# Interleaved memory attention and multi-head attention: the kernel without its filler matmuls on TensorE

## The chip, the cores and the metric

The kernel runs on one core of a Trainium2 chip. The metric is the device time in microseconds of one execution, as the median of several runs. The engines have short names here: PE is TensorE, ACT is ScalarE, DVE is VectorE, POOL is GpSimd, SP is SyncE. "The granted clock" is the share of TensorE's full clock that the chip let it have, as the trace records it.

## The reference

Four layers run one after another on x of 2048 tokens by 512 features in bf16: A, B, A, B. Each is a residual block on a layer-normalised input. There are 32 heads of 16 features.

```python
def A(x):                                  # memory attention, 4 segments of 512 tokens
    for s in range(4):
        p = softmax(q_s @ k_s.T * scale + causal_mask)      # inside the segment
        a_dot = p @ v_s
        num, den = phi(q_s) @ M, phi(q_s) @ z + 1e-6        # memory of earlier segments
        o = g * num / den + (1 - g) * a_dot
        M, z = M + phi(k_s).T @ v_s, z + sum(phi(k_s))
    return concat(outs) @ wo

def B(x):                                  # full attention over 2048 keys
    p = softmax(q @ k.T * scale)
    return (p @ v) @ wo

x = x + A(layernorm(x)); x = x + B(layernorm(x))            # layers 1, 2
x = x + A(layernorm(x)); x = x + B(layernorm(x))            # layers 3, 4
```

The work that counts is the exponential: 32 heads by 2048 by 2048 in each B layer, and a quarter of that, less the blocks above the diagonal, in each A layer.

## The kernel before

The program is laid out at build time by a scheduler written in Python. It keeps a modelled time for each engine (`sc.t["pe"]`, `sc.t["act"]`, ...), picks the next piece of work in a loop, and emits it into that engine's instruction stream. On the chip the engines then run their streams and wait for one another by semaphores. The code counts layers from 0, so `L` is 0 to 3.

Scores come in tiles of 128 keys by 512 queries, one PSUM bank each. Three tiles make a group: three matmuls, then one exponential on ACT over 1536 columns into a ring in SBUF (`pT`). Two sets of three banks alternate, so that PE fills one set while ACT reads the other:

```python
    # emit_group (cut)
    sc.add("pe", lambda e: e.matmul(out, lhsT, rhs, start=True, stop=True), ..., name="S",
           cost=((SC0 if k == 0 else N / 2400.0) if i == 0 else SC1),
           cold=N / 2400.0 if i == 0 else 0.0, work=0.14 * N / 512)          # line 1113
    ...
    o = sc.add("act", lambda e: e.activation(dst, src, ACT.Exp, scale=float(SCALE)), ...,
               name="E", cost=0.065 + W / 1200.0)                            # line 1120
```

Part of the score tiles of the B layers, four at a time, go to DVE instead, which works out the exponential in eight steps on 128x2048 after moving each tile out of PSUM (line 1249). Weighted sums of values follow, on line 1376 with the values stationary, and on line 1358 with the probabilities stationary (layers `L` 2 and 3; 17 columns each). All projections, the memory products and the output projections pass through one helper (line 610), mostly as groups of four accumulating matmuls.

The scheduler has a model of PE's clock. It adds up the matmul work in windows of `HAM_W` us, and takes PE to be warm if the window before had at least `HAM_T`; a matmul in a cold window costs more in the model:

```python
HAM_W = 3.4133
HAM_T = 5.0
KEEP = 6.0
KEEP0 = 3.0
KEEP_D = 0.0
KEEP_L = 2
CF = 0.684

    def clock(self, t, work):
        w = int(t / HAM_W)
        if w > self.win:
            self.warm = w == self.win + 1 and self.work >= HAM_T
            self.win, self.work = w, 0.0
        self.work += work
        self.past.append((t, work))
        while self.past[0][0] < t - HAM_W:
            self.past.popleft()
        return self.warm

    # add() (cut)
        if eng == "pe" and not self.clock(t0, work):
            cost += CF * cold
```

When the loop finds nothing ready for PE, it moves PE's modelled time on to the next event. Before it does so, it may put in a filler: a matmul of zeros, added to the accumulation that is open at that moment, so that no result changes. `rs`, `rp` and `rx` are the times at which the next score group, value sum and DVE tile become ready:

```python
    # end of run()'s loop
            to = min(nxt)
            d = 0.23 if sc.warm else 0.44
            tc = min([x for x in (rs, rp, rx) if x is not None], default=to)
            if KEEP and self.acc_open and t + d <= tc + KEEP_D and (0.0 if sc.warm else KEEP0) <= sc.lately() < KEEP and self.pvu and self.pvu[0]["L"] <= KEEP_L:
                self.keep_warm()
                continue
            sc.t["pe"] = to

    def keep_warm(self):

        bank = self.acc_bank
        self.sc.add("pe", lambda e: e.matmul(self.ps[:, bank.col0:bank.col0 + 512], self.zw[:, :], self.wA[:, 0, 0:512], start=False, stop=False,
                                             skip_group_check=True),
                    reads=[self.b_zw, self.b_wA[0]], bank_ops=[(bank, "w", self.acc_alloc)], emit=False, name="D", cost=0.215, cold=0.2133, work=1.0)   # line 1826
```

`sc.lately()` is the work of the last `HAM_W` us. `KEEP_L = 2` keeps fillers out of the last layer.

Of the kernel before, what the change touches and what calls it, by code (L numbers as in the profile page):

```python
# [37 lines left out]
LAST = 3  # L38
HAM_W = 3.4133
HAM_T = 5.0  # L40
KEEP = 6.0
KEEP0 = 3.0
KEEP_D = 0.0
KEEP_L = 2
# [239 lines left out]
class KernelBuilder:  # L284
# [1444 lines left out]
    def run(self):  # L1729
# [3 lines left out]
        while True:  # L1733
# [83 lines left out]
# [3 lines that stand above are left out]
# [80 lines left out]
```

## Time and profile before

| what | value |
|---|---|
| time, median of 3 runs | 2110.33 us (2109.41 to 2111.07) |
| span of the profiled run | 2108.4 us |
| mean granted TensorE clock | 0.670 |
| busy ACT / PE / DVE / POOL | 1996.9 / 1737.0 / 1608.0 / 253.4 us |
| exponentials on ACT (line 1120) | 1504, 1962.6 us |
| score tiles that go to DVE (line 1249) | 420, that is 105 times four |
| filler matmuls (line 1826) | 126, 53.0 us |

A line of the page's groups names the source line, the engine and operation, what it writes and reads, how many there are, then busy time and the mean length of one, and then how long the engine stood idle just before them and who ended that. [...] Layers follow one another, but not sharply: the scheduler mixes units of two layers.

### The profile page before, as it was taken

To read this page: it belongs to the slowest core of one execution; us is meant where nothing else is said; L and a number is where in the kernel's file an instruction comes from. 1 tells how busy PE (TensorE), PEld (TensorE's weight loads), DVE (VectorE), ACT (ScalarE), POOL (GpSimd) and SP (SyncE) were. 2 spreads that over 40 slices of the span, in tenths; PEclk is the share of its full clock that TensorE was granted. 3 is DMA by queue.
4 is the path that set the end of the run, shared out by engine and by line. 5 is a ranking of instruction groups with operands and counts; after the bars stand their busy time and mean duration, and the time that the engine had idled before them with its cause. 6 is when DMAs were issued, how large, how long until landed. Compare 5 with 4: busy or idle time off the path is not lost.

```text
span 2108.4 us, 41713 instructions
## 1 busy us (share of the span) xinstructions
PE 1737.0 (82%) x17508; PEld 597.9 (28%) x17508; DVE 1608.0 (76%) x2449; ACT 1996.9 (95%) x1593; POOL 253.4 (12%) x564
## 2 busy tenths in 40 slices
PE   6879978887878787878888888888888888888887
PEld 2222221112231122221232223213444433434443
DVE  7887558876648768777767678578789878988894
ACT  6869889999999999999999998999999999999998
POOL 4542220000130003110021102200000000000000
PEclk9779876568575796577875797575655555556555
DMA  4210100001000000010000100000000000000000
GB/s 120 51 31 20 22 11 1 1 1 21 1 11 11 6 16 1 1 21 11 11 1 1 19 13 1 14 8 2 14 4 4 4 14 4 4 5 14 5 6 12
DMA packets 75468, 27.33 MB, mean 13 GB/s; under 512 B 68112, under 2 KB 74768, under 8 KB 75280
## 3 DMA queue, kind: packets, MB, share of 16 engines
q1 hardware_dynamic: 74176, 23.62, 5.4%
q8 instruction: 137, 2.24, 0.4%
q10 hardware_dynamic: 1104, 1.05, 0.1%
q14 instruction: 51, 0.42, 0.1%
HBM read 6.30 MB, written 2.10 MB: 4 GB/s over the span
## 4 chain that ended last, share of the span: by engine, by line
ACT 46%; PE 26%; issue 10%; DVE 4%; POOL 1%; DMA 0%; SPq 0%; ACTq 0%; DVEq 0%
ACT pT L1120 45%; PE ps L1113 11%; PE ps L610 6%; PE ps L1358 4%; PE ps L1376 3%; PE ps L1246 1%; POOL pT L1143 1%; DVE dz L1249 1%; DMA xT<-xn 0%; PE ps L1826 0%; ACT et L765 0%; DVE db L1304 0%; DVE dz L1302 0%; DVE db L1293 0%; DVE tokk L1302 0%
## 5 line engine op out<-in xcount | busy, mean ns | idle before, releaser
L1120 ACT ACTIVATE pT<-ps 128x1536 bf16<-128x1536 f32 (+1 forms) x1504 | 1962.6, 1494 | 85.3 <-PE ps L1113 68.8
L1113 PE MATMUL ps<-q,kB 32*128 32x512 bf16 x3676 | 680.4, 535 | 264.5 <-ACT pT L1120 256.4
L1249 DVE TENSOR_SCALAR dz<-ps 128x512 int32<-128x512 f32 x420 | 289.8, 690 | 148.0 <-PE ps L1246 135.7
L1113 PEld LDWEIGHTS ps<-q,kB 32*128 32x128 bf16 x3676 | 129.2, 97 | 691.0 <-ACT pT L1120 645.7
L1143 POOL TENSOR_SCALAR_AFFINE_SELECT pT<-pT 128x256 bf16<-128x256 bf16 (+2 forms) x516 | 224.6, 464 | 544.7 <-ACT pT L1120 543.4
L1376 PE MATMUL ps<-pT,vB 128*17 128x512 bf16 x2228 | 271.3, 491 | 3.8 <-DVE kB L625 1.3
L1246 PE MATMUL ps<-q,kB 32*128 32x512 bf16 x420 | 238.7, 568 | 0.2 <-DVE dz L1249 0.2
L1358 PEld LDWEIGHTS ps<-vB,pT 128*128 128x128 bf16 x5792 | 181.0, 104 | 165.1 <-issue 163.9
L1358 PE MATMUL ps<-vB,pT 128*128 128x17 bf16 x5792 | 213.7, 176 | 0.0
L1113 PE MATMUL ps<-q,kA 32*128 32x128 bf16 (+3 forms) x1024 | 122.2, 381 | 41.9 <-ACT pT L1120 39.6
L1286 DVE TENSOR_SCALAR df<-dz 128x2048 f16<-128x2048 uint16 x105 | 129.2, 1230 | 2.9
L1376 PEld LDWEIGHTS ps<-pT,vB 128*17 128x17 bf16 x2228 | 51.3, 89 | 189.2 <-issue 174.3
L1293 DVE TENSOR_SCALAR db<-dz 128x2048 int16<-128x2048 int16 x77 | 94.3, 1225 | 0.5 <-PE ps L1376 0.5
L1496 DVE STREAM_TRANSPOSE T<-ps 128x512 f32<-128x512 f32 x94 | 66.7, 709 | 28.4 <-PE ps L1376 27.8
L610 PE MATMUL ps<-xT,wB 128*128 128x512 bf16 x256 | 81.5, 452 | 5.3 <-DMA xT<-xn 2.5
L610 PE MATMUL ps<-xT,wA 128*128 128x512 bf16 x256 | 72.5, 412 | 6.0 <-DVE T L1496 2.6
L655 POOL TENSOR_SCALAR lnr<-lnmv 128x4 f32<-128x4 f32 x15 | 6.0, 403 | 565.5 <-DVE lnmv L650 565.5
L976 DVE TENSOR_TENSOR x_tok<-x_tok,ps 128x512 bf16<-128x512 bf16 x60 | 41.0, 686 | 42.6 <-PE ps L610 42.2
L1298 DVE TENSOR_TENSOR tokk<-tokk,df 128x2048 f16<-128x2048 f16 x56 | 68.3, 1220 | 0.8
L1302 DVE TENSOR_TENSOR tokk<-tokk,df 128x2048 f16<-128x2048 f16 x56 | 68.3, 1219 | 0.8
L665 DVE TENSOR_SCALAR xn<-x_tok,lnmv,lnr 128x512 bf16<-128x512 bf16 x60 | 25.3, 442 | 54.6 <-DMA xT<-xn 52.2
L1113 PEld LDWEIGHTS ps<-q,kA 32*128 32x128 bf16 x1024 | 29.8, 99 | 120.8 <-ACT pT L1120 95.3
(130 smaller groups left out, 1613.4 us busy)
## 6 DMA issues: line engine op xcount, KB each, us to landing
x_tok<-in_A_x_dram SPq DMA_DIRECT2D x14, 128.0 KB, 2.7
wB<-in_B_wqkv_dram SPq DMA_DIRECT2D x4, 384.0 KB, 4.4
out_dram<-x_tok SPq DMA_DIRECT2D x3, 512.0 KB, 3.6
xT<-xn SPq DMA_TRANSPOSE x60, 2.4
wA<-in_A_wk_dram SPq DMA_DIRECT2D x1, 512.0 KB, 5.5
wA<-in_A_wq_dram ACTq DMA_DIRECT2D x1, 512.0 KB, 6.8
wA<-in_A_wv_dram SPq DMA_DIRECT2D x1, 512.0 KB, 7.0
woA<-in_A_wo_dram SPq DMA_DIRECT2D x1, 512.0 KB, 6.8
```

Of the source, the lines that this page charges most:

```text
L610: return self.sc.add("pe", lambda e: e.matmul(out, lhsT, rhs, start=start, stop=stop), reads=reads, bank_ops=[(bank, "w", alloc)], emit=la ...
L1113: sc.add("pe", (lambda out, lhsT, rhs: lambda e: e.matmul(out, lhsT, rhs, start=True, stop=True))(out, lhsT, rhs), reads=reads, bank_ops=[ ...
L1120: o = sc.add("act", lambda e: e.activation(dst, src, ACT.Exp, scale=float(SCALE)), writes=[self.b_pT[s0 + i] for i in range(n)], bank_ops= ...
L1143: om = sc.add("pool", (lambda ap, pat: lambda e: e.affine_select(ap, ap, pattern=pat, compare_op=ALU.is_ge, fill=0.0, base=0, channel_mult ...
L1246: sc.add("pe", lambda e: e.matmul(out, lhsT, rhs, start=True, stop=True), reads=reads, bank_ops=[(bank, "w", alloc)], emit=True, name="SX" ...
L1249: o = sc.add("dve", lambda e: e.tensor_scalar(dst, out, float(EXP_C * 65536.0), -126.0 * 65536.0, op0=ALU.mult, op1=ALU.max), writes=[self ...
L1286: o = dv(lambda e: e.tensor_scalar(F, lo, 2.0 ** -16, -0.5, op0=ALU.mult, op1=ALU.add), bz, bF, "dF", 1.24)
L1293: o = dv(lambda e: e.tensor_scalar(E, hi, 128.0, 16256.0 + 53.0, op0=ALU.mult, op1=ALU.add), bz, bE, "dE", 1.24)
L1298: o = dv(lambda e: e.tensor_tensor(Pz, Pz, F, ALU.mult), bF + bP, bP, "dP2", 1.24)
L1302: o = dv(lambda e: e.tensor_tensor(Pz, Pz, F, ALU.mult), bF + bP, bP, "dP4", 1.24)
L1358: op = sc.add("pe", (lambda o0, w, v, first: lambda e: e.matmul(self.ps[:, o0:o0 + 17], w, v, start=first, stop=True, skip_group_check=Tru ...
L1376: sc.add("pe", (lambda out, v, rhs, start, stop: lambda e: e.matmul(out, v, rhs, start=start, stop=stop, skip_group_check=True))(out, v, r ...
```

## The change

One constant is changed: `KEEP`, the amount of recent work up to which fillers are put in, goes from 6.0 to zero. The condition is then never met and no filler is emitted. The version after is described as: layer 3 memory attention queries-stationary, wide query masks, four Z sums early, projection of the last segment accumulated early, new unit order. All of that stands in both kernels; the fillers, which are for keeping PE's clock up in the first three layers, are the whole difference in the source. The scheduler runs with the same rules and all its other constants, on a PE timeline that has no fillers in it.

```diff
--- before.py
+++ after.py
@@ -38,7 +38,7 @@
 LAST = 3
 HAM_W = 3.4133
 HAM_T = 5.0
-KEEP = 6.0
+KEEP = 0.0
 KEEP0 = 3.0
 KEEP_D = 0.0
 KEEP_L = 2
```

## The prediction, made before the result was known

> **What bounds the kernel now.** I read the page first: the busy shares, then the strip of 40 slices. ScalarE (ACT) is busy for 1996.9 us of 2108.4; nothing else is near it.
>
> ```profile
> PE 1737.0 (82%) x17508; PEld 597.9 (28%) x17508; DVE 1608.0 (76%) x2449; ACT 1996.9 (95%) x1593; POOL 253.4 (12%) x564
> ...
> PE   6879978887878787878888888888888888888887
> ...
> ACT  6869889999999999999999998999999999999998
> ...
> PEclk9779876568575796577875797575655555556555
> ```
>
> The ACT strip is at 9 from slice 7 on (from about 320 us), while the granted TensorE clock swings between full and half in slices 7 to 25 and lies at half from slice 29 to the end, with ACT still at 9. So the clock, which is all that the filler matmuls are there for, does not by itself set the pace. The loss is in 111 us of ACT idle time, so next I read the groups of ACT by shape and the waits.
>
> ```profile
> L1120 ACT ACTIVATE pT<-ps 128x1536 bf16<-128x1536 f32 x1312 | 1800.3, 1559 | 62.9 <-PE ps L1113 49.7 <-POOL pT L1143 5.9 <-PE ps L1246 4.9
> ```
>
> ```profile
> PE ps L1113 <- ACT pT L1120: 295.9, 726, 1.5
> ...
> ACT pT L1120 <- PE ps L1113: 68.8, 64, 10.1
> ```
>
> PE waits for ACT 726 times and ACT for PE 64 times. Those 64 waits are what a warmer or colder PE can change. The last view is of the object of the change, the filler of line 1826, alone, and then of whole stretches of 50 us (columns: span of the stretch, busy us and count of PE, PEld, DVE, ACT, POOL, then granted clock, DMA share, GB/s).
>
> ```profile
> L1826 PE MATMUL ps<-wA,zw x126: 376/390/634, 113.3 to 1294.5; 128*128 128x512 bf16 x126
> ```
>
> ```profile
> 400.00:450.00 50.00, 41.09 (x255) 7.69 (x251) 43.79 (x55) 49.94 (x39) 0.00 (x0) 0.53 0.00 1
> ...
> 750.00:800.00 50.00, 39.62 (x302) 12.05 (x301) 35.31 (x74) 50.00 (x43) 3.59 (x5) 0.95 0.04 9
> ...
> 1600.00:1650.00 50.00, 42.47 (x655) 20.65 (x651) 45.28 (x56) 50.00 (x38) 0.00 (x0) 0.50 0.02 4
> ```
>
> There are 126 fillers, all between 113 and 1295 us; 71 ran at the full clock and 55 at half (durations under and over 450 ns). The stretch 750 to 800 us has 17 of them, the most of any, and ACT has no gap in it: fillers can sit beside the work for nothing. The stretch 400 to 450 us has 5, and the clock is 0.53 all the same. The stretch 1600 to 1650 us has none, the clock is at half, and ACT has no gap either.
>
> [...] its clock record holds only 0.50 and 1.00, changing on a grid of 3.413 us. [...] the trace has medians of 379 ns for warm projection matmuls and 602 ns for the score matmuls (mostly cold)[...]. [...] the trace shows 78 of them without a gap in 105.54 us (from 611 us on), so 1353 ns each. That last number is the kernel's beat: three score tiles in 1.353 us of ACT.
>
> **The change part by part.** With KEEP at zero the branch that emits the filler is never taken.
>
> *Removed:* 126 matmuls of 512 columns. In a row, four projection matmuls start 658 / 3 = 219 ns apart at full clock and 1252 / 3 = 417 ns at half (median first-to-fourth start distances of the groups of line 610). So the fillers hold the array for 71 x 0.22 + 55 x 0.42 = 38.7 us. PE was waiting for ACT 296 us in the whole run, and the scheduler puts a filler only where its own model shows an empty slot. The chain that ended last has 0.5% (10 us) on line 1826, but much of this lies in stretches where ACT has no gap, like 750 to 800 us; there nothing is gained. I take 1 to 2 us as the direct gain.
>
> *Lost:* warm windows. For every window of 3.413 us I added up the matmuls of the trace, a full 128x128 matmul of 512 columns counting as 1 and the others by their share of array and columns (the 17-column ones of line 1358 left out). Under 4, the next window was warm in 2 of 352 cases; from 4 to 6 in 51 of 110; over 6 in 151 of 152. Fillers stand in 63 windows. Without them 45 of the 63 fall below 4.5, and 28 of these were followed by a warm window. So some 28 windows, or 96 us, may go cold: the mean granted clock would fall from 0.670 by 96 x 0.5 / 2108 = 0.023, to about 0.647. What counts is what runs in those 28 windows: 6 projection groups of four. Each takes 1252 - 658 = 594 ns longer, 3.6 us of PE in sum. How much of that reaches ACT? Around 1346 us a cold group (1.89 us) before a score group makes the exponential wait 0.88 us, and this 0.88 comes back many times; about half of the cold groups show no such gap. From 340 to 1295 us 17 of 98 groups are cold, and ACT is idle 24.3 us from all causes. So 6 x 0.88 x 0.5 to 6 x 0.88, that is 2.6 to 5.3 us, and as much as 1 us for the memory products of lines 610 (136 columns) in those windows. I take 4 us as the direct loss.
>
> *Moved:* the program's order. Scheduling is done at build time against a model of each engine, which counts a cold matmul dearer, so once the first filler is gone (113 us) every later choice may fall otherwise: which of two ready units comes first, when a projection is squeezed in, how many quadruples of score tiles go to VectorE (now 105). One quadruple more or less is 4 x 1.353 / 3 = 1.8 us of ACT. The 10.08 us wait near 141 us, and those of 4.5 us near 310 us, 4.1 us near 802 us and 3.0 us near 913 us, sit at joints between segments and can each shrink or grow. The other constants (unit order, rate, look-ahead) are shared by both kernels. If they were chosen for the present order, a shuffle more often hurts than helps; I book +2 us, with a spread of about 10.
>
> *Sum:* 2110.3 - 1.5 + 4 + 2 = about **2115 us**.
>
> **The rivals.**
> *Fillers in the way.* Each cold filler is 0.42 us ahead of a score group in PE's program order. If the 10 us that the chain puts on line 1826 were all delay, the change would give 2100. For it: the model's clock is not the chip's, and 55 fillers ran at the slow price though the model hoped for the fast one. Against it: 726 waits of PE for ACT, and no ACT gap in the stretch with most fillers.
> *The clock is worth more than I count.* If each window that the fillers warm keeps the next warm too, perhaps 20 instead of 6 projection groups turn cold, and memory products and layer normalization wait for them at the joints: 20 x 0.88 = 18 us, so 2128. Against it: in most of the 28 windows no projection follows at all, and the projections bring their own activity (four in one window are already 4 of the 5 that the scheduler asks for).
> *Only the shuffle.* Clock and fillers cancel and the new order decides, by one or two quadruples and one joint: 2095 to 2130, either sign.
>
> **Range and chances.** The direct terms are a few us; the shuffle gives the width. I take 2098 to 2132 us for 8 in 10. Two per cent is 42 us: more than a third of all ACT idle time won, or that much lost. Winning it needs ACT work to shrink as well, so 1% for faster, 4% for slower, 95% for within 2%.
>
> **What would show it.** Right: line 1826 is gone; the mean clock falls to 0.63 to 0.66, with slices 7 to 25 lower; ACT busy time stays within 6 us of 1996.9; ACT's waits on line 1113 grow by 2 to 8 us from 68.8; the count of L1249 stays near 420. Wrong: an ACT idle time that shrinks at a lower clock would speak for fillers in the way; a changed L1249 count with ACT busy following at 1.8 us for each four, for the shuffle; many new waits of 0.88 us behind line 610, for the dearer clock. A whole new wait at a joint, over 5 us, would be a miss that I can't foresee from this trace.

## The result and the profile after

The changed kernel takes 2093.86 us (2089.86 to 2096.14) against 2110.7 us: a ratio of 0.9915, with a 95% interval of 0.9896 to 0.9935. It is faster by 0.85%, some 18 us. The prediction was 2115 us in a range of 2098 to 2132, so both the sign and the range were wrong; the 95% given to a change within 2% held.

The page of the changed kernel, busy shares and strips:

```profile
PE 1732.3 (83%) x17382; PEld 589.3 (28%) x17382; DVE 1605.0 (77%) x2447; ACT 1997.3 (95%) x1595; POOL 248.1 (12%) x563
...
ACT  5879989999999999999999999999999999999998
...
PEclk9779876567565575576765788575655565555555
```

ACT does the same work as before, 1997.3 us against 1996.9, in a span that is 14 us shorter (2094.3 against 2108.4). PE has 126 matmuls less and its clock fell from 0.670 to 0.643, as foreseen. So all that was won is ACT idle time. The exponentials over 1536 columns, which before stood behind 62.9 us of idle time, and ACT's longest waits:

```profile
L1120 ACT ACTIVATE pT<-ps 128x1536 bf16<-128x1536 f32 x1312 | 1800.4, 1551 | 52.7 <-PE ps L1113 46.3 <-POOL pT L1143 1.7 <-PE ps L1246 1.7
```

```profile
ACT pT L1120 <- PE ps L1113: 59.3, 59, 6.8
...
ACT pT L1120 <- POOL pT L1143: 4.7, 6, 2.1
```

The count stays (1312), the idle time falls by 10 us, and the longest wait is 6.8 us, in the first 20 us of the program, where it was 10.1, at the first joint. The stretches of 50 us (same columns as in the prediction):

```profile
400.00:450.00 50.00, 41.60 (x259) 7.27 (x255) 45.65 (x55) 49.93 (x39) 0.00 (x0) 0.50 0.00 1
750.00:800.00 50.00, 40.72 (x306) 11.41 (x306) 36.46 (x77) 49.94 (x42) 6.02 (x16) 0.66 0.04 9
1600.00:1650.00 50.00, 42.09 (x660) 20.72 (x657) 45.04 (x55) 49.94 (x38) 0.00 (x0) 0.50 0.02 5
```

From 750 to 800 us the clock is 0.66 in place of 0.95, and ACT is as full as before (49.94 us busy against 50.00). Where, then, do the 18 us come from? The next table follows the progress of ACT: for each share of all exponential columns, the time at which it was done in the two traces. The difference moves in steps, not evenly:

| time in the kernel before, us | 46 | 125 | 210 | 281 | 768 | 834 | 1259 | 1394 | 2100 |
|---|---|---|---|---|---|---|---|---|---|
| changed minus before, us | +2.9 | +4.7 | -0.3 | -4.1 | -4.0 | -8.3 | -7.1 | -16.0 | -15.6 |

There are three steps, of about 9, 4 and 9 us, with little between them and nothing in the last 700 us, where neither kernel has fillers. A second trace of the changed kernel (run e9 below) has the same three steps, of about 10, 4 and 9 us. The first two are joints: places where an output projection or a quadruple of DVE tiles has to be finished before the next unit goes on. The third is not one long wait. Its stretch of work, in the kernel before and then in the changed one (columns: span of the stretch, busy us and count of ACT, granted clock, DMA share, GB/s):

```profile
1259.00:1394.00 135.00, 121.21 (x109) 0.68 0.05 10
```

```profile
1252.00:1378.00 126.00, 120.32 (x108) 0.76 0.05 10
```

ACT is idle 13.8 us of it before and 5.7 us after. The longest wait shrinks only from 4.10 to 3.29 us; of the shorter waits, nine of 0.3 us and more become two. Among these, five of about 0.88 us, the length that the prediction tied to cold projection groups, become two. The changed kernel, without fillers, has the higher clock here. The first joint on ACT in the kernel before (start, length, instruction, idle time before it and who ended it):

```profile
138.10 0.63 ACT L765 ACTIVATE et<-tokk 128x512 bf16<-128x512 bf16 x1 [2.03 <-DVE sm L899]
140.76 0.63 ACT L765 ACTIVATE et<-tokk 128x512 bf16<-128x512 bf16 x1 [2.03 <-DVE sm L899]
151.47 2.37 ACT L1120 ACTIVATE pT<-ps 128x1536 bf16<-128x1536 f32 x2 [10.08 <-PE ps L1113]
```

And in the changed kernel:

```profile
138.84 1.02 ACT L1120 ACTIVATE pT<-ps 128x1024 bf16<-128x1024 f32 x1 [3.28 <-PE ps L1113]
...
145.47 0.63 ACT L765 ACTIVATE et<-tokk 128x512 bf16<-128x512 bf16 x1 [2.32 <-DVE sm L899]
149.82 3.71 ACT L1120 ACTIVATE pT<-ps 128x1536 bf16<-128x1536 f32 x3 [3.72 <-PE ps L1113]
```

Here the scheduler must finish the output projection of segment 0 before it can reuse a buffer, and issues no scores until that is done. In the plan (the modelled order and times that the scheduler works out) that takes eight steps of its threads in the old order and five in the new; a 10 us hole becomes two of under 4 us.

The second joint, all engines, in the kernel before:

```profile
794.88 0.38 PE L1246 MATMUL ps<-q,kB 32*128 32x512 bf16 x1
...
796.03 1.23 DVE L1286 TENSOR_SCALAR df<-dz 128x2048 f16<-128x2048 uint16 x1
...
804.18 0.39 PE L1376 MATMUL ps<-db,vB 128*17 128x512 bf16 x4 [2.43 <-DVE db L1304]
...
806.36 2.79 ACT L1120 ACTIVATE pT<-ps 128x1536 bf16<-128x1536 f32 x2 [4.12 <-POOL pT L1143]
```

And in the changed kernel:

```profile
782.19 0.63 PE L1246 MATMUL ps<-q,kB 32*128 32x512 bf16 x1
...
783.59 1.23 DVE L1286 TENSOR_SCALAR df<-dz 128x2048 f16<-128x2048 uint16 x1
...
791.24 0.61 PE L1376 MATMUL ps<-db,vB 128*17 128x512 bf16 x4 [0.24 <-DVE db L1304]
...
801.68 5.48 ACT L1120 ACTIVATE pT<-ps 128x1536 bf16<-128x1536 f32 x4 [0.92 <-PE ps L1113]
```

The last of four tiles for DVE is scored at 794.9 us in the old order and 782.2 us in the new. The DVE chain takes about 8 us, and the last value sum of that unit must wait for it (2.43 us against 0.24). The value sums of the next unit stand behind it, and the next scores after them: ACT stops for 4.12 us. The profile names POOL as the releaser. POOL was late too, for its causal masks meet the same DVE chain here and not in the new order (a mask takes 0.77 us on average from 796 to 808 us, and 0.42 in the same stretch of work of the changed kernel). Which of the two makes the joint is the question of the last experiment.

### The profile page after: what moved, and what is told of

Same layout as the page of the kernel before. It is cut to its first block, busy times and chain, and to the rows that moved or that the text cites. A ratio compares the mean times of both kernels' runs of the same rounds, so it can differ in the third digit from the quotient of the medians.

```text
span 2094.3 us, 41469 instructions
## 1 busy us (share of the span) xinstructions
PE 1732.3 (83%) x17382; PEld 589.3 (28%) x17382; DVE 1605.0 (77%) x2447; ACT 1997.3 (95%) x1595; POOL 248.1 (12%) x563
## 4 chain that ended last, share of the span: by engine, by line
ACT 48%; PE 30%; issue 10%; DVE 9%; POOL 1%; DMA 1%; SPq 0%; ACTq 0%; DVEq 0%; POOLq 0%
ACT pT L1120 47%; PE ps L1113 12%; PE ps L610 8%; PE ps L1358 5%; PE ps L1376 4%; PE ps L1246 2%; POOL pT L1143 1%; DMA xT<-xn 1%; DVE T L1496 1%; DVE lnst L647 1%; DVE dz L1249 1%; DVE ot L904 0%; DVE ph L771 0%; SPq L429 0%; DVE df L1286 0%
## 5 line engine op out<-in xcount | busy, mean ns | idle before, releaser
L1120 ACT ACTIVATE pT<-ps 128x1536 bf16<-128x1536 f32 (+1 forms) x1504 | 1962.6, 1487 | 69.0 <-PE ps L1113 59.3
L1113 PE MATMUL ps<-q,kB 32*128 32x512 bf16 x3676 | 696.0, 548 | 262.3 <-ACT pT L1120 254.5
L1249 DVE TENSOR_SCALAR dz<-ps 128x512 int32<-128x512 f32 x420 | 289.8, 690 | 153.5 <-PE ps L1246 139.5
L1376 PE MATMUL ps<-pT,vB 128*17 128x512 bf16 x2228 | 286.0, 515 | 2.3 <-DVE ot L904 1.3
L1143 POOL TENSOR_SCALAR_AFFINE_SELECT pT<-pT 128x256 bf16<-128x256 bf16 (+2 forms) x515 | 219.5, 455 | 549.2 <-ACT pT L1120 547.9
L1246 PE MATMUL ps<-q,kB 32*128 32x512 bf16 x420 | 243.3, 579 | 0.0
L1113 PE MATMUL ps<-q,kA 32*128 32x512 bf16 (+3 forms) x1024 | 125.0, 391 | 40.4 <-ACT pT L1120 38.6
L625 DVE CAST q<-ps 128x512 bf16<-128x512 f32 x53 | 36.4, 686 | 34.5 <-PE ps L610 34.4
```

Source lines behind the costliest of these rows:

```text
L1113: sc.add("pe", (lambda out, lhsT, rhs: lambda e: e.matmul(out, lhsT, rhs, start=True, stop=True))(out, lhsT, rhs), reads=reads, bank_ops=[ ...
L1143: om = sc.add("pool", (lambda ap, pat: lambda e: e.affine_select(ap, ap, pattern=pat, compare_op=ALU.is_ge, fill=0.0, base=0, channel_mult ...
L1249: o = sc.add("dve", lambda e: e.tensor_scalar(dst, out, float(EXP_C * 65536.0), -126.0 * 65536.0, op0=ALU.mult, op1=ALU.max), writes=[self ...
L1376: sc.add("pe", (lambda out, v, rhs, start, stop: lambda e: e.matmul(out, v, rhs, start=start, stop=stop, skip_group_check=True))(out, v, r ...
```

## The experiments

**The fillers alone, and the order alone.** The theory after the trace: the new order wins and the fillers themselves weigh little. Two rivals: the fillers were in the way; or the clock is worth much and hid behind a better order. The first two experiments change one thing each. The first keeps the old plan and leaves the planned fillers out of the program:

```diff
-        for op in self.ops[eng_name]:
+        for op in [o for o in self.ops[eng_name] if o.name != "D"]:
```

> The scheduler plans with its 126 filler matmuls as in the kernel before, and the fillers alone are left out of the program, so every other instruction stands where it stood in the kernel before. Theory 'new order' (the re-planned program is better, the fillers themselves weigh nothing): 2105 to 2114 us. Rival 'fillers in the way' (each filler holds up a score group): 2094 to 2100 us, nearly all of the 17 us won. Rival 'clock worth much' (masked in the changed kernel by a better order): slower than 2115 us, with a mean clock near 0.645.

Measured: 2112.72 us, ratio 0.9993 (0.9986 to 0.9999), clock 0.644. All instructions of DVE, ACT and POOL are those of the kernel before in the same order. The waits at the joints are all there without a filler in the program, even a little longer:

```profile
154.94 2.37 ACT L1120 ACTIVATE pT<-ps 128x1536 bf16<-128x1536 f32 x2 [10.41 <-PE ps L1113]
```

```profile
807.53 2.79 ACT L1120 ACTIVATE pT<-ps 128x1536 bf16<-128x1536 f32 x2 [5.31 <-POOL pT L1143]
```

The second keeps the new order and puts 103 fillers into idle places of its plan, which are charged nothing there:

```diff
+            while self.quiet and t + d <= tc and self.acc_open and self.pvu and self.pvu[0]["L"] <= KEEP_L:
+                x = sc.lately() + sum(1 for a in self.quiet if a >= t - HAM_W)
+                if not (0.0 if sc.warm else KEEP0) <= x < 6.0:
+                    break
+                self.quiet.append(t)
+                self.keep_warm()          # appended to PE's stream only
+                t += d
             sc.t["pe"] = to
```

> The program of the changed kernel, order untouched, with 103 fillers put into places where its plan has PE idle and an accumulation open, by the rule of the kernel before; the plan counts no time and no work for them. Theory 'new order': 2090 to 2098 us, the time of the changed kernel, with a mean clock back near 0.66. Rival 'fillers in the way': 2104 to 2112 us. Rival 'clock worth much': under 2088 us.

Measured: 2091.38 us, ratio 0.9891 (0.9878 to 0.9903), clock 0.668. DVE, ACT and POOL have the changed kernel's instructions in its order. Together the two settle the main point. The old order without fillers is as slow as with them (to 0.07%), and the new order with fillers is as fast as without, or a little faster. "Fillers in the way" falls by both: nothing like 17 us was won by the first or lost by the second.

**Where the order is drawn.** The next two allow fillers only in one part of the plan's time, and so give a third and a fourth plan.

```diff
-            if KEEP and self.acc_open ...
+            if KEEP and t < 340.0 and self.acc_open ...      # e3
+            if KEEP and t >= 340.0 and self.acc_open ...     # e4
```

> Fillers are allowed only while the plan's time is under 340 us: 17 of them; the plan is that of the kernel before up to there and a third one after. Theory 'new order': the 9 us that the changed kernel wins between 125 and 281 us are missing here, the rest is drawn afresh, so 2098 to 2112 us, with the first 280 us as in the kernel before. Rival 'fillers in the way': 15 of 17 us won, near 2096 us, as 109 fillers of 126 are gone. Rival 'clock worth much': no prediction apart from the first.

Measured: 2119.34 us, ratio 1.0021 (1.0012 to 1.0030): slower than the kernel before and outside what was expected, with 17 fillers left of 126. "Fillers in the way", which gave 2096 us, falls here too.

> Fillers are allowed only from 340 us of the plan's time on: 159 of them; the plan is that of the changed kernel up to there and a fourth one after. Theory 'new order': the first 340 us as in the changed kernel, so 4 us ahead of the kernel before at 281 us, then drawn afresh: 2092 to 2110 us. Rival 'fillers in the way': 159 fillers after 340 us cost what 109 cost before and more, so 2108 to 2114 us. Rival 'clock worth much': faster than the changed kernel, under 2090 us.

Measured: 2109.64 us, ratio 0.9980 (0.9970 to 0.9990). This time lies in the ranges of two theories, so it alone does not decide between them. The progress of ACT, each minus the kernel before:

| time in the kernel before, us | 125 | 281 | 768 | 834 | 1014 | 1079 | 1259 | 1394 | 2100 |
|---|---|---|---|---|---|---|---|---|---|
| changed kernel | +4.7 | -4.1 | -4.0 | -8.3 | -7.9 | -9.2 | -7.1 | -16.0 | -15.6 |
| e1, old order, no fillers | +3.4 | +3.0 | -0.7 | +1.2 | +2.8 | +2.9 | +5.6 | +3.7 | +2.7 |
| e2, new order, fillers | +3.3 | -5.0 | -7.9 | -12.1 | -11.8 | -12.6 | -12.1 | -20.1 | -20.1 |
| e3, fillers to 340 us | +2.5 | +2.7 | +2.1 | +6.8 | +7.6 | +7.1 | +7.6 | +5.4 | +6.4 |
| e4, fillers from 340 us | +2.5 | -6.3 | -4.1 | -7.5 | -7.9 | +1.2 | +3.4 | +1.0 | -4.6 |

As the theory has it, e4 takes the first step (it shares the new order there) and e3 does not. After that each plan has its own luck at the joints: e3 loses 5 us at 768 to 834 us, where the changed kernel wins 4; e4 loses 9 us at 1014 to 1079 us, where no other in the table does: one place and not, as fillers in the way would have it, wherever fillers are. The number of tiles that go to DVE moves as well, 416 in e3 and 428 in e4 against 420; a quadruple is 1.8 us of ACT.

The scheduler's own forecast goes with this. Its modelled time at the end of the program, "the plan's end", is 2089.4 us for the kernel before, 2075.7 for the changed one, 2096.6 for e3 and 2085.7 for e4: the same sequence as on the chip, 18 to 24 us lower. Its modelled waits of ACT are at the measured places too (9.6 us at 139, 3.9 at 796 us in the kernel before).

**Is a plan without fillers better as such, or only with these constants?** Two other constants of the scheduler were moved slightly, each with and without fillers. They change the order and, a little, the share of DVE: 424, 432, 424 and 428 tiles in e5 to e8, against 420.

```diff
-RATE = 0.762
+RATE = 0.77          # e5 with KEEP = 0.0, e6 with KEEP = 6.0
```

> The changed kernel (no fillers) with RATE 0.77 in place of 0.762, which alters only how often the scheduler squeezes in other work. Its plan ends at 2104.7 us, against 2075.7 for the changed kernel and 2089.4 for the kernel before. Theory 'the order decides, and the shared constants suit the plan without fillers': measured time is the plan's end plus 18 to 24 us, so 2122 to 2129 us, slower than the kernel before though it has no fillers. Rival 'a plan without fillers is better as such': 2090 to 2100 us.

Measured: 2121.80 us, ratio 1.0043 (1.0030 to 1.0056).

> The kernel before (with fillers, here 193 of them) with RATE 0.77. Its plan ends at 2080.0 us. Theory 'the order decides': 2098 to 2104 us, so with this rate taking the fillers out costs 1.2%, the reverse of the change studied. Rival 'a plan without fillers is better as such': 2108 to 2118 us, slower than the same rate without fillers.

Measured: 2106.58 us, ratio 0.9970 (0.9959 to 0.9981). The sign is as expected; the time is 2.6 us above the range given.

```diff
-DVE_AHEAD = 4.525
+DVE_AHEAD = 4.51     # e7 with KEEP = 0.0, e8 with KEEP = 6.0
```

> The changed kernel with DVE_AHEAD 4.51 in place of 4.525 (15 ns of look-ahead). Its plan ends at 2116.8 us. Theory 'the order decides': 2134 to 2142 us. Rival 'a plan without fillers is better as such': 2090 to 2100 us.

Measured: 2134.07 us, ratio 1.0098 (1.0083 to 1.0113).

> The kernel before with DVE_AHEAD 4.51; 178 fillers. Its plan ends at 2079.0 us. Theory 'the order decides': 2097 to 2103 us, 1.8% faster than the same constant without fillers. Rival 'a plan without fillers is better as such': 2108 to 2118 us.

Measured: 2105.96 us, ratio 0.9965 (0.9951 to 0.9978); the sign as expected, 3 us above the range. The waits of ACT on its scores, e7 and then e8:

```profile
ACT pT L1120 <- PE ps L1113: 98.4, 65, 10.8
```

```profile
ACT pT L1120 <- PE ps L1113: 73.9, 73, 6.6
```

e7 waits less often than e8 and loses 24 us more: three of its waits, near 814, 1225 and 1316 us, are over 10 us each, again at joints. With either constant, taking the fillers out makes the kernel slower, by 0.7% (2121.80 against 2106.58) and by 1.3% (2134.07 against 2105.96): the reverse of the change studied. A part of this is work moved to DVE: ACT is busy 1996.0 us in e5 and 1990.8 in e6, but 1993.7 and 1993.8 in e7 and e8. ACT idle time makes up the rest: 123.6 against 114.0 us, and 137.9 against 111.3. So a plan without fillers is not better as such.

**What the fillers are worth by themselves.** The changed kernel once more, beside its own order with 103 fillers (the edit of e2) and with 346 (a filler in every idle place of the plan while an accumulation is open):

```diff
-                if not (0.0 if sc.warm else KEEP0) <= x < 6.0:
+                if x >= 16.0:                                    # e11
```

> The changed kernel once more, beside the next two on the same chip. All theories: 2090 to 2097 us.

> The changed kernel's order with 103 fillers in its idle places, as in the second experiment, now beside the changed kernel itself. Theory 'fillers weigh nothing': the same ratio to the kernel before as the changed kernel, within 0.1%. Rival 'the warmer clock is worth a few us, and the fillers cost less than that': 0.1 to 0.3% faster than the changed kernel, about 2090 us. Rival 'fillers in the way': slower than it.

> The changed kernel's order with a filler in every idle place that its plan shows while an accumulation is open, 346 of them. Mean clock 0.70 or more. Theory 'fillers weigh nothing': 2090 to 2097 us. Rival 'warmer clock worth a few us': 2082 to 2089 us, faster than with 103. Rival 'fillers in the way': over 2100 us, as cold fillers of 0.42 us outgrow the idle places that the plan assumed.

| kernel | fillers | clock | median, us | ratio (95% interval) |
|---|---|---|---|---|
| e9 | 0 | 0.649 | 2095.97 | 0.9908 (0.9895 to 0.9922) |
| e10 | 103 | 0.664 | 2091.02 | 0.9891 (0.9875 to 0.9906) |
| e11 | 346 | 0.676 | 2091.44 | 0.9899 (0.9885 to 0.9912) |

With fillers the same order comes out 0.1 to 0.2% faster, and e2 pointed the same way, but the intervals overlap; three times as many fillers do no more. A small use of the warmer clock, up to some 4 us, is possible and not settled. The new order with 103 fillers is thus the fastest median of all, 2091 us, but not shown to be faster than the changed kernel.

**The second joint: the late quadruple or the slowed masks.** The kernel before with the same plan, but with masks of 8 columns in place of 128 in its second memory attention layer, so that most of that layer's causal mask is left out:

```diff
+                w = 8 if tiles[i]["u"]["L"] else 128
 ...
-                    pat = [[0, 2], [1, 128]]
+                    pat = [[0, 2], [1, w]]          # and likewise for the other patterns
```

> The kernel before with the same plan, but in its second memory attention layer each causal mask covers 8 of its 128 columns, so most of the causal mask of that layer is left out and POOL has a sixteenth of the mask work there. Its masks take 0.85 to 1.38 us near 800 us in place of 0.41, while the DVE chain runs. Theory 'the late DVE quadruple makes the second joint': PE still waits for the chain until about 804 us, so ACT's wait of 4.12 us near 802 us shrinks by no more than 1 us, and the whole kernel gains 1 to 3 us: 2107 to 2112 us. Rival 'the slowed masks make it': that wait falls under 1.5 us and the kernel gains 3 to 6 us.

Measured: 2111.15 us, ratio 0.9991 (0.9983 to 0.9999). The whole gain, some 2 us, is in the range expected. The hole at the second joint stays:

```profile
810.42 2.79 ACT L1120 ACTIVATE pT<-ps 128x1536 bf16<-128x1536 f32 x2 [3.79 <-PE ps L1113]
```

It shrinks from 4.12 to 3.79 us only, and PE is now named as releaser. The edit does not take all of the masks' time away, since short masks, too, are slow where the DVE chain runs: 13 of them take 7.05 us where the full ones took 10.10. But the last of them ends at 808.4 us, and PE waits for the last DVE step until 808.2 us (1.82 us of waiting):

```profile
808.21 0.61 PE L1377 MATMUL ps<-db,vB 128*17 128x512 bf16 x4 [1.82 <-DVE db L1305]
```

(The line numbers are one higher in this kernel.) The missing scores start at 809.6 us, 1.3 us after the last mask. So the slowed masks do not make this joint. The difference of 0.3 us is of single traces, and the same order had 5.31 us in e1. That the late DVE quadruple makes it is read from PE's wait in the traces; no run moves the quadruple alone. The naming of POOL in the kernel before meant that it came last, not that it was the cause.

## Why the prediction was wrong, point by point

**What bounds the kernel: right.** ACT's work is the same to 0.4 us, and a stretch at half clock (0.50) such as 1600 to 1650 us leaves it full in both kernels (50.00 and 49.94 us busy of 50). (Slice 25 of its strip is 8, not 9 as all after slice 7 were said to be.)

**Removed (-1 to -2 us) and lost (+4 us for the clock): small, as said; their sum had the wrong sign in the old order.** With the order kept, leaving the fillers out gains 0.07% (0.01 to 0.14%), 1.5 us of 2113. That figure holds both terms, the gain and the loss by the colder clock, and the runs do not part them: booked at +2.5 us, they measure -1.5. In the new order leaving them out comes out 4 us dearer by the ratios of e9 and e10, which is not clear of noise. The rival "fillers in the way" was rightly discounted, but one argument for it was misread: the scheduler did not hope for the full clock in all fillers. Its plan charges 62 of the 126 the cold price, and 55 ran at half clock.

The clock itself was foreseen well: 0.647 predicted, 0.643 measured, and 0.644 in e1. Here a clock of 0.676 against 0.649 (e11 against e9, same order) comes out at 0.1%, with overlapping intervals. That fits with PE waiting for ACT 293 us (745 waits) in the changed kernel.

**Moved (+2 us, "a shuffle more often hurts", spread about 10): this is the step that failed.** The order is worth 0.9915 / 0.9993 = 0.9922, that is -16 us where +2 was booked: the wrong sign, and beyond the spread of 10 that I gave. The number of quadruples did not change (420 tiles in both); what moved are the waits of ACT, 111.5 us of idle time before and 97.0 after. Two things were wrong in the step. First, I took for granted that the shared constants had been chosen for the order of the kernel before. e5 to e8 speak for the opposite: at 0.762 and 4.525 the plan without fillers is unusually good, and a step of 0.008 or 0.015 in either constant throws it 28 to 40 us back, while the plan with fillers gets 4 to 7 us faster. The scheduler's modelled times, which are not measured ones, say the same over more values. Without fillers the plan's end is 2075.7 us at each value of RATE tried from 0.750 to 0.764; with them it is 2086.1 at 0.754, 2096.0 at 0.760, 2089.4 at 0.762 and 2080.0 at 0.77. In 300 plans each, with RATE, DVE_AHEAD, DX_AHEAD and DX_SLACK drawn at random within 0.02, 0.1, 0.05 and 0.1 of their values, the median plan's end is 2099 us without fillers and 2095 with them. One of the 300 without fillers ends before 2075.7. So the changed kernel's plan is among the best of its kind, which is how constants look that were tuned without fillers. That they were in fact tuned so is an inference. For a reader of the trace of the kernel before, which way the order falls is luck. Second, I took the spread too small: I named the waits at the joints (10.08, 4.1 us and others) but the rival "only the shuffle" counts on one joint, where two joints and the stretch from 1259 us on moved in the same direction. That they did is luck too, as far as the runs show.

**The rivals.** "Only the shuffle" was the right mechanism, with 2095 to 2130 as its range and the result 1 us outside it. Its quadruples did not move, but its joint did. "Fillers in the way" and the dear clock are both excluded at the size that they were given (10 and 18 us) by e1, which has no fillers, a clock of 0.644 and the old order's time.

**The signs.** Line 1826 gone, clock 0.63 to 0.66, ACT busy within 6 us, L1249 at 420: all came. ACT's waits on line 1113 were to grow by 2 to 8 us and fell by 9.5, from 68.8 to 59.3. "An ACT idle time that shrinks at a lower clock" was to speak for fillers in the way; e1 and e2 show that this reading was wrong: the idle time follows the order (115.4 us in e1, 93.4 in e2), not the fillers.

**What stays open.** The runs show no reason why the plan with fillers comes out worse at all three places, other than chance and the choice of the constants. How much of the third step is order and how much is the higher clock of that stretch is not parted. And whether the fillers are worth 0.2% in a good order is not settled.

## What to carry to other kernels

When a program is laid out by a scheduler at build time, an edit to any of its constants can make a new program. Split its effect in two before judging it: the old order with the new instructions, and the new order with the old ones. A helper that loses under constants tuned without it has not been shown useless (here the sign turns with a constant moved by 0.3%), and for a kernel bound by one engine, look for the gain in that engine's waits before the clock of another: here ACT, busy for 95% of the span, stood idle 14.5 us less in all while PE's clock fell from 0.670 to 0.643.

## What the runs showed that I had not expected

The scheduler's plan forecasts well which program is faster, but it favours fillers. Measured time minus plan's end:

| kernel | fillers | plan's end | measured | difference |
|---|---|---|---|---|
| changed | 0 | 2075.7 | 2093.9 | 18.2 |
| e5 | 0 | 2104.7 | 2121.8 | 17.1 |
| e7 | 0 | 2116.8 | 2134.1 | 17.3 |
| before | 126 | 2089.4 | 2110.7 | 21.3 |
| e3 | 17 | 2096.6 | 2119.3 | 22.7 |
| e4 | 159 | 2085.7 | 2109.6 | 23.9 |
| e8 | 178 | 2079.0 | 2106.0 | 27.0 |
| e6 | 193 | 2080.0 | 2106.6 | 26.6 |

Without fillers the difference is 17 to 18 us (20.3 in e9), with them 21 to 27. The rows are of different series, and the kernel before varied from 2110.7 to 2113.8 us between these; e5 to e8 are of one series, and there it is 17 against 27. The difference goes with the plan and not with the fillers on the chip: e1, planned with fillers and run without, has 23.3, and e2, planned without and run with 103, has 15.7. Why is open. That the plan takes the fillers for warm does not explain it: it charges the cold price to 62 of the 126 in the kernel before, where 55 ran at half clock, and to 74 of the 193 in e6, where 61 did.

POOL's masks take longer beside DVE's wide steps. A mask of 128x256 has a median of 0.41 us in the kernel before, but those that meet DVE's 128x2048 steps near 800 us take 0.85 to 1.38 us, close to the length of the DVE step itself (0.78 to 1.31). The 16-column masks of e12 speak for waiting and not for slower work: a median of 0.22 us, and up to 1.19 where the DVE chain runs.

```profile
L1144 POOL TENSOR_SCALAR_AFFINE_SELECT pT<-pT x15: 189/221/1192, 800.0 to 811.9; 128x16 bf16<-128x16 bf16 x11, 128x24 bf16<-128x24 bf16 x2, 128x8 bf16<-128x8 bf16 x2
```

(Minimum, median and maximum in ns.) Six of these masks, of 0.64 to 1.19 us, start within a DVE step of 0.72 to 1.26 us, and each ends less than 0.1 us after that step. In the kernel before, the six masks of 128x256 that start within such a step from 797 to 804 us end 0.26 to 0.27 us after it. So these masks seem to be held until the step is done; by what, the traces do not show.
